# Units of 384 tokens for the third product of a fused float32r kernel, with a*b in pieces of 384 and 192 columns

## The chip, the cores and the metric

The kernel runs on one core of one Trainium2 chip. The metric is the device time of one execution in microseconds, lower is better. The chip is driven by five engines: TensorE (PE; its weight loads are listed apart as PEld), VectorE (DVE), ScalarE (ACT), GpSimd (POOL) and SyncE (SP), whose queue issues most of the DMAs.

## The reference

Three stages follow each other. Attention with 32 packed queries gives x of 8 batches of 576 tokens (4608 tokens in all) by 512 features; then a gated product, then a leaky one:

```
p_packed = softmax(p k^T / 8) v
x   = softmax(q p_packed^T / 8) p_packed
x   = ((x w1) * (x w2)) w3 w_out
h   = x w_in
out = max(0.01 h, h) w_out2
```

The products with d_ff = 1024 and 2048 are in float32.

## The kernel before

Tokens lie along the free dimension. W13 = w3 w_out (1024 x 512) is made once at the start. Float32 precision comes from float32r pairs: a number is split into hi (a cast on ACT) and lo = x - hi (a subtraction on DVE), and `three` (L128 to L130) issues three matmuls for a product: hi*hi, hi*lo, lo*hi. Each of these matmuls has a weight load of 128 x 128 ahead of it.

The first part runs batch by batch. Of batch b:

- **a*b** (`ab_unit`): 16 pieces, 8 blocks fc of 128 hidden features times two halves th of 288 tokens. A piece is 12 matmuls of 288 columns, M (weights) by AT (moving): 6 into one PSUM tile (a), 6 into another (b). ACT copies a to SBUF (`ab_a`), DVE multiplies (`ab_mul`), ACT casts hi (`ab_hi`), DVE subtracts (`ab_lo`). PSUM has four tiles `mm`, so two pieces are in flight.
- **x2** (`x2_unit`): for each half th four units e, each 24 matmuls (8 blocks fc, three passes) of 288 columns, W13 by ab. ACT copies the result to `x2s` and stores it to `x2d` in DRAM (`x2_store`).
- Beside these 16 + 8 slots (`slots`) stand the steps of attention for batch b+1 (`attention`: loads, scores s1 at slot 1, transposes at 7, pv at 10, pp at 13, scores s2 at 16, the softmax s2 and the split of AT at 16 to 21, and at 21 `m_pair`, the first two M = w pp of the next batch, on PE, cast on ACT and subtracted on DVE), the conversion of w_in and w_out2 from float64 words (`pump`, `conv_flush`), and staging.
- **Staging** (`stage_att`, L546 to L552 in `form`): for a unit of 768 tokens and one half a of the features it loads four tiles from `x2d` into buffers `v`, forms sums and hi and lo parts of seven operands (11 DVE operations, 7 casts on ACT into two buffers `P`), and stores them to `xfd` with 14 DMAs. One stage stands in each of the batches 2 to 6.

The second part (from L775 in `run`) multiplies the staged forms by w_in and w_out2, in matmuls of 384 columns, in a scheme of seven products.

Batch 0 follows an order written out by hand (`SCRIPT`); from batch 1 on the instructions are recorded in the order of the slots, and a scheduler places them on each engine. Each engine and each DMA queue then works its list in order: an instruction that waits holds those behind it.

Of the kernel before, what the change touches and what calls it, by code (L numbers as in the profile page):

```python
# [36 lines left out]
F32 = mybir.dt.float32  # L37
F32R = mybir.dt.float32r
# [17 lines left out]
def tile_kernel(ctx, tc, qT, kT, vL, pT, w12, w3b, wo1, win, wo2, out):  # L56
    nc = tc.nc
# [4 lines left out]
    x2d = dram.tile([P, 4, NT], F32, name="x2d")  # L62
# [17 lines left out]
    def ps_mm():  # L80
        return psum["pool"].tile([P, 512], F32, tag="mm", name="mm", bufs=3 if psum["early"] else 4)
# [11 lines left out]
    main = stA.enter_context(tc.tile_pool(name="main", bufs=1, side="right"))  # L93
# [5 lines left out]
    W13 = main.tile([P, 8, 2, DM], F32R, name="W13")  # L99
# [138 lines left out]
    def s2_mm(b):  # L238
        s2q[b] = scores(ppT[b % 2], "q", b)
# [151 lines left out]
    Mp, Mt, abp, ab32, abt, x2p = {}, {}, {}, {}, {}, {}  # L391
    mark = {"a": [], "v": []}
# [13 lines left out]
        m = Mt[b, f]  # L406
        sub(nc.vector, m[:, 1], Mp.pop((b, f)), m[:, 0])

    def half_tile(th):
        return main.tile([P, 2, TH], F32R, tag=f"ab{th}", name="ab", bufs=8)  # L410

    def ab_mm(b, fc, th):
        m = Mt[b, fc // 2]
        pair = ps_mm(), ps_mm()
        for w in range(2):
            c = fc % 2 * 256 + w * P
            for g in range(2):
                at = ATs[b, g]
                three(
                    pair[w][:, :TH], lambda i: m[:, i, g, c:c + P], lambda i: at[:, i, th * TH:(th + 1) * TH],  # L420
                    g == 0, g == 1,
                )
        abp[fc, th] = pair

    def ab_a(fc, th):
        pa, pb = abp[fc, th]
        a = main.tile([P, TH], F32, tag="a", name="a", bufs=2)
        nc.scalar.copy(a, pa[:, :TH])
        abp[fc, th] = a, pb

    def ab_mul(fc, th):
        a, pb = abp.pop((fc, th))
        t = main.tile([P, TH], F32, tag="ab32", name="ab32", bufs=3)
        nc.vector.tensor_tensor(out=t, in0=pb[:, :TH], in1=a, op=ALU.mult)  # L434
        ab32[fc, th] = t

    def ab_hi(fc, th):
        t = half_tile(th)
        mark["a"].append(nc.scalar.copy(t[:, 0], ab32[fc, th]))  # L439
        abt[fc, th] = t  # L440

    def ab_lo(fc, th, engine=nc.vector):
        t = abt[fc, th]
        mark["v"].append(sub(engine, t[:, 1], ab32.pop((fc, th)), t[:, 0]))

    def x2_mm(b, th, e):
# [4 lines left out]
        x2p[b, th, e] = ps  # L451

    def x2_store(b, th, e):
        t = main.tile([P, TH], F32, tag="x2s", name="x2s", bufs=2)
        nc.scalar.copy(t, x2p.pop((b, th, e))[:, :TH])
        nc.scalar.dma_start(out=x2d[:, e, b * S + th * TH:b * S + (th + 1) * TH], in_=t)

    AB = [(2 * f + n, th) for f in range(4) for th in range(2) for n in range(2)]
    X2 = [(th, e) for th in range(2) for e in range(4)]

    def m_pair(b, f):
        m_mm(b, f)
        m_mm(b, f + 1, False)
        for x in (f, f + 1):
            m_hi(b, x)
            m_lo(b, x)

    def ab_unit(b, fc, th):
# [106 lines left out]
    def stage_att(u, a):  # L575

        def tile(tag, bufs):
            return lambda: att.tile([P, HT], F32, tag=tag, name=tag, bufs=bufs)

        return stage(u, a, tile("v", VB), tile("PT", 2), lambda: tile("P", 2)().bitcast(F32R))  # L580

    def spread(steps, first, last):
        d = {}
        for n, f in enumerate(steps):
            d.setdefault(first + n * (last - first + 1) // len(steps), []).append(f)
        return d
# [13 lines left out]
        "U": x2_mm, "Us": x2_store, "P": ps_late,  # L600
# [25 lines left out]
    for b in range(1, 7):
        staging = {}
        if b in STAGE:
            steps = stage_att(*STAGE[b])
            staging = spread(steps[1:], 16, 23)  # L630
            staging[12] = steps[:1]
        slots(enumerate(pieces(b)), rest_of_m(b), attention(b + 1), pumps(PUMPS[b]), staging)
# [228 lines left out]
    for t in range(TB):  # L861
# [29 lines left out]
        if end:  # L891
# [3 lines left out]
            if t + 1 < TB:  # L895
                n = len(evicted)
# [45 lines left out]
```

## Time and profile before

| | before |
|---|---|
| time, median of 3 runs | 1265.77 us (1264.15 to 1268.5) |
| profiled execution, its own time | 1268.98 us |
| its span, first to last instruction | 1266.2 us |
| TensorE busy (share of the span) | 1245.5 us (98%) |
| weight loads busy | 1167.7 us (92%) |
| VectorE busy | 871.2 us (69%) |
| ScalarE busy | 610.4 us (48%) |
| GpSimd busy | 112.9 us (9%) |
| granted TensorE clock, mean | 0.999 |
| HBM traffic | 222 GB/s over the span |

Busy is the time in which at least one instruction of the engine was running. A matmul's recorded duration holds its latency, so consecutive matmuls overlap in the records; what one costs in a stream is read from starts, as the chain view gives it (a stretch divided by its count). Batches 1 to 6 lie between about 143 and 508 us of the span.

### The profile page before, as it was taken

Reading aid. Unit: us, or ns where it says so; the run is one execution under the profiler, and the core shown is the slowest. Engines: PE = TensorE matmul, PEld = TensorE weight load, DVE = VectorE, ACT = ScalarE, POOL = GpSimd, SP = SyncE. Lnnn points to the kernel's source line nnn. Section 1 sums busy time; section 2 is a strip of 40 time slices with the busy share of each in tenths; the row PEclk is TensorE's granted clock in tenths of the full one; section 3 lists DMA queues with packets and bytes.
Section 4 is the critical chain, followed back from the end, with each engine's and each line's share of the span. In section 5 each row is a group of like instructions: output and inputs, shape, how many; then the busy total and the mean of one; then the engine's idle time right before and its main releaser. Section 6 shows DMA issues by size and latency. Waiting matters only on the chain.

```text
span 1266.2 us, 23462 instructions
## 1 busy us (share of the span) xinstructions
PE 1245.5 (98%) x8984; PEld 1167.7 (92%) x8984; DVE 871.2 (69%) x1448; ACT 610.4 (48%) x1125; POOL 112.9 (9%) x136
## 2 busy tenths in 40 slices
PE   7989999999999999999999999999999999999998
PEld 2458898989889999999999999999999999999998
DVE  7887465767675767639866773886467448776667
ACT  4354345454545454546655655563433434443433
POOL 6553011111120200000000000000000000000000
PEclk9999999999999999999999999999999999999999
DMA  9954253767583835468788777284744674698883
GB/s 366 352 186 138 69 175 126 243 195 255 169 277 113 286 119 173 148 223 295 251 304 308 278 268 241 96 294 184 275 147 177 225 250 149 231 346 293 297 294 126
DMA packets 139952, 283.09 MB, mean 224 GB/s; under 512 B 14912, under 2 KB 67136, under 8 KB 139840
## 3 DMA queue, kind: packets, MB, share of 16 engines
q1 hardware_dynamic: 130624, 272.16, 61.9%
q10 hardware_dynamic: 9216, 9.44, 2.2%
q8 instruction: 70, 1.15, 0.4%
q14 instruction: 42, 0.34, 0.1%
HBM read 202.38 MB, written 79.17 MB: 222 GB/s over the span
## 4 chain that ended last, share of the span: by engine, by line
PE 94%; DMA 4%; DVE 1%; issue 0%; ACT 0%; SPq 0%; DVEq 0%; ACTq 0%
PE mm L130 31%; PE b L775 31%; PE c L775 16%; PE a L775 8%; PE at L164 3%; PE mm L379 3%; DMA c<-w3b 1%; DMA v<-x2d 1%; PE at L221 1%; DMA M<-w3b 1%; PE at L204 1%; DMA xl<-xfd 0%; DVE cT L283 0%; DMA c<-w 0%; DVE ct L280 0%
## 5 line engine op out<-in xcount | busy, mean ns | idle before, releaser
L130 PEld LDWEIGHTS mm<-AT,M 128*128 128x128 f32 x1536 | 205.5, 188 | 16.8 <-ACT ab L439 10.0
L130 PE MATMUL mm<-AT,M 128*128 128x288 f32 x1536 | 215.4, 297 | 3.4 <-DVE M L135 1.5
L775 PE MATMUL b<-xh,wi 128*128 128x384 f32 x768 | 216.6, 335 | 0.0
L775 PE MATMUL b<-gh,wo 128*128 128x384 f32 x768 | 215.1, 335 | 0.0
L130 PEld LDWEIGHTS mm<-ab,W 128*128 128x128 f32 x1536 | 203.7, 188 | 9.5 <-issue 6.1
L130 PE MATMUL mm<-ab,W 128*128 128x288 f32 x1536 | 207.8, 295 | 0.0
L775 PEld LDWEIGHTS b<-xh,wi 128*128 128x128 f32 x768 | 140.5, 188 | 0.0
L775 PEld LDWEIGHTS b<-gh,wo 128*128 128x128 f32 x768 | 140.4, 188 | 0.0
L775 PE MATMUL b<-xl,wi 128*128 128x384 f32 x384 | 128.4, 334 | 0.0
L775 PE MATMUL b<-gl,wo 128*128 128x384 f32 x384 | 128.3, 334 | 0.0
L550 ACT CAST gh<-gr 128x1152 fp32r<-128x1152 f32 (+1 forms) x72 | 75.7, 1053 | 77.5 <-PE b L775 48.0
L775 PE MATMUL c<-gh,wo 128*128 128x384 f32 x384 | 106.4, 334 | 0.0
L775 PE MATMUL c<-xh,wi 128*128 128x384 f32 x384 | 105.3, 334 | 0.0
L135 DVE TENSOR_TENSOR gl<-gr,gh 128x1152 fp32r<-128x1152 f32 (+1 forms) x72 | 87.9, 1220 | 15.8 <-ACT gh L550 15.8
L434 DVE TENSOR_TENSOR ab<-mm,a 128x288 f32<-128x288 f32 x128 | 58.0, 455 | 52.4 <-PE mm L130 32.8
L727 DVE TENSOR_TENSOR o<-b,o 128x384 f32<-128x384 f32 x108 | 59.3, 553 | 33.8 <-PE b L775 33.5
L550 ACT CAST gh<-gs 128x1152 fp32r<-128x1152 f32 (+1 forms) x54 | 56.9, 1054 | 45.7 <-PE b L775 27.2
L439 ACT CAST ab<-ab 128x288 fp32r<-128x288 f32 x128 | 55.4, 433 | 47.9 <-DVE ab L434 47.7
L735 ACT COPY gr<-b 128x384 f32<-128x384 f32 x96 | 45.9, 480 | 66.8 <-PE b L775 66.6
L721 ACT ACTIVATE gr<-gr 128x1152 f32<-128x1152 f32 (+1 forms) x54 | 57.3, 1061 | 42.3 <-DVE gr L727 42.1
L135 DVE TENSOR_TENSOR ab<-ab,ab 128x288 fp32r<-128x288 f32 x119 | 54.7, 459 | 32.2 <-ACT ab L439 30.7
L775 PEld LDWEIGHTS b<-xl,wi 128*128 128x128 f32 x384 | 72.1, 188 | 0.0
(119 smaller groups left out, 2045.7 us busy)
## 6 DMA issues: line engine op xcount, KB each, us to landing
xh<-xfd SPq DMA_DIRECT2D x126, 384.0 KB, 5.5
xl<-xfd SPq DMA_DIRECT2D x126, 384.0 KB, 5.2
part<-o SPq DMA_DIRECT2D x48, 384.0 KB, 2.7
o<-part SPq DMA_DIRECT2D x48, 384.0 KB, 6.4
xfd<-xt SPq DMA_DIRECT2D x49, 192.0 KB, 3.0
xfd<-xr SPq DMA_DIRECT2D x49, 192.0 KB, 3.0
raw<-kT SPq DMA_DIRECT2D x32, 288.0 KB, 5.3
raw<-qT SPq DMA_DIRECT2D x32, 288.0 KB, 4.0
```

The costliest lines, as they stand in the source:

```text
L130: ins = nc.tensor.matmul(dst, lhs(i), rhs(j), start=first and n == 0, stop=last and n == 2)
L135: return engine.tensor_tensor(out=out, in0=x, in1=rd(hi), op=ALU.subtract)
L164: ins = nc.tensor.matmul(dst(h)[c * 32:c * 32 + 32], lhs[r, c, :], rhs(c)[r], start=True, stop=True)
L204: together(nc.tensor.transpose(t[:, 0, c * P:(c + 1) * P], pt[:, c:512:4], ident), g + c == 0)
L379: nc.tensor.matmul(w13p[fc], words["3", i][:, c:c + P], words["o", jc], start=w13n[fc] == 1, stop=w13n[fc] == 8)
L434: nc.vector.tensor_tensor(out=t, in0=pb[:, :TH], in1=a, op=ALU.mult)
L439: mark["a"].append(nc.scalar.copy(t[:, 0], ab32[fc, th]))
L550: gate("a", nc.scalar.copy(hi[step], x[step]))
L721: nc.scalar.activation(out=out, in_=x, func=AF.Prelu, alpha=0.01)
L727: evicted.append(nc.vector.tensor_tensor(**args))
L735: nc.scalar.copy(out, ps)
L775: ins = nc.tensor.matmul(dst, lhs(l), rhs(r), start=first and n == 0, stop=last and n == total - 1, skip_group_check=True)
```

## The change

Batches 1 to 6 are 3456 tokens, nine units of 384. x2 is now computed per unit: one unit in batches 1, 3 and 5 (the first 384 of their tokens), two in batches 2, 4 and 6 (the rest of the batch before with the first 192 of this one, then the last 384). a*b is cut to fit: an odd batch into pieces of 384 and 192 columns, an even one into 192 and 384. An odd batch so has 16 + 4 slots, an even one 16 + 8. Attention for the next batch, the pumps and `m_pair` are moved to earlier slots in odd batches. Staging is taken out of odd batches; batch 4 and batch 6 have two stages. AT has two buffers in place of four; `x2s` shares three buffers with `a`. Batches 0 and 7 keep halves of 288.

```
-        at = main.tile([P, 2, S], F32R, tag="AT", name="AT", bufs=4)
+        at = main.tile([P, 2, S], F32R, tag="AT", name="AT", bufs=2)
...
+    WIDE = 384
+    CUTS = {b: ((0, 384, 576) if b % 2 else (0, 192, 576)) if 0 < b < 7 else (0, 288, 576) for b in range(B)}
...
+    def piece_of(b, fc, th):
+        c0, c1 = CUTS[b][th:th + 2]
+        if 0 < b < 7:
+            unit, at = divmod((b - 1) * S + c0, WIDE)
+        else:
+            unit, at = (b, th), 0
+        if unit not in sets:
+            sets[unit] = sides[0], {}
+            sides[0] ^= 1
+        side, tiles = sets[unit]
+        if fc not in tiles:
+            tiles[fc] = half_tile(side)
+        return tiles[fc], slice(at, at + c1 - c0)
...
     def ab_mm(b, fc, th):
...
+        c0, c1 = CUTS[b][th:th + 2]
...
-                    pair[w][:, :TH], lambda i: m[:, i, g, c:c + P], lambda i: at[:, i, th * TH:(th + 1) * TH],
+                    pair[w][:, :c1 - c0], lambda i: m[:, i, g, c:c + P], lambda i: at[:, i, c0:c1],
...
-        a = main.tile([P, TH], F32, tag="a", name="a", bufs=2)
+        a = main.tile([P, WIDE], F32, tag="a", name="a", bufs=3)[:, :n]
...
+    def x2_mm(unit, e):
+        n = TH if isinstance(unit, tuple) else WIDE
         ps = ps_mm()
         for fc in range(8):
-            t = abt[fc, th]
-            three(ps[:, :TH], lambda i: W13[:, fc, i, e * P:(e + 1) * P], lambda i: t[:, i], fc == 0, fc == 7)
+            t = sets[unit][1][fc]
+            three(ps[:, :n], lambda i: W13[:, fc, i, e * P:(e + 1) * P], lambda i: t[:, i, :n], fc == 0, fc == 7)
...
+    def units(b):
+        if b % 7 == 0:
+            return [(b, 0), (b, 1)]
+        return [3 * (b // 2)] if b % 2 else [3 * (b // 2) - 2, 3 * (b // 2) - 1]
...
+        first = 14 if short else 16
...
-        d[16] += [lambda: s2_mm(b)]
+        d[first] += [lambda: s2_mm(b)]
...
-        d[21] += [lambda: m_pair(b, 0)]
+        d[18 if short else 21] += [lambda: m_pair(b, 0)]
...
-        for s in (5, 10, 14, 18, 20, 22)[:n]:
+        for s in ((5, 9, 12, 15, 17, 19) if short else (5, 10, 14, 18, 20, 22))[:n]:
...
-    PUMPS = (0, 6, 6, 6, 5, 5, 4)
-    STAGE = {2: (0, 0), 3: (0, 1), 4: (1, 0), 5: (1, 1), 6: (2, 0)}
+    PUMPS = (0, 6, 5, 6, 4, 6, 5)
+    STAGE = {2: ((0, 0),), 4: ((0, 1), (1, 0)), 6: ((1, 1), (2, 0))}
...
+        short = b % 2 == 1
...
+            first, last = ((16, 19), (20, 23))[n]
+            staging.setdefault((12, 19)[n], []).extend(steps[:1])
```

Over the whole program the float32r matmuls of batches 1 to 6 were 2304 of 288 columns (1152 of a*b, 1152 of x2); they are now 576 of 384 and 576 of 192 in a*b, and 864 of 384 in x2. On PE, from the last pieces of batch 1 to the first of batch 2 (`ppT` and `raw` are the scores s2, `w` and `ppT` the M of the next batch), before:

```order
L130 MATMUL mm<-AT,M 128x288 x36
L130 MATMUL mm<-ab,W_76 128x288 x24
L164 MATMUL at<-raw,ppT_77 32x288 x16
L130 MATMUL mm<-ab,W_76 128x288 x120
L164 MATMUL at<-w,ppT_77 32x512 x16
L130 MATMUL mm<-ab,W_76 128x288 x48
L130 MATMUL mm<-AT,M 128x288 x24
```

and now:

```order
L130 MATMUL mm<-AT,M 128x384 x12
L130 MATMUL mm<-AT,M 128x192 x12
L164 MATMUL at<-raw,ppT_77 32x288 x16
L130 MATMUL mm<-AT,M 128x192 x12
L130 MATMUL mm<-ab,W_76 128x384 x72
L164 MATMUL at<-w,ppT_77 32x512 x16
L130 MATMUL mm<-ab,W_76 128x384 x24
L130 MATMUL mm<-AT,M 128x192 x12
```

Between the scores and the next batch stood 120 + 48 matmuls of 288 columns and the M; now 12 of 192, 72 + 24 of 384 and the M.

On DVE in batch 4, where the first sum of a stage (`PT<-v`) stands after the multiplication of the first piece behind pv, before:

```order
L434 TENSOR_TENSOR ab_4527<-mm,a 128x288
L135 TENSOR_TENSOR ab<-ab_4527,ab 128x288
L546 TENSOR_TENSOR PT<-v 128x384
L434 TENSOR_TENSOR ab_4549<-mm,a 128x288
L135 TENSOR_TENSOR v<-v,P 128x384
```

and now:

```order
L457 TENSOR_TENSOR ab_4230<-mm,a 128x384
L582 TENSOR_TENSOR PT<-v 128x384
L457 TENSOR_TENSOR ab_4252<-mm,a 128x192
L135 TENSOR_TENSOR v<-v,P 128x384
L135 TENSOR_TENSOR ab<-ab_4230,ab 128x384
```

The sum stands at the same place, between the multiplications of the first and the second piece.

On DVE at the end of batch 4, from the last steps of the softmax s2 to the first a*b of batch 5, before:

```order
L258 TENSOR_TENSOR sT<-sT,st_4766 128x576
L260 STREAM_TRANSPOSE a_4762<-sT 128x576
L135 TENSOR_TENSOR AT<-a_4762,AT 128x576
L260 STREAM_TRANSPOSE a_4858<-sT 128x576
L280 TENSOR_SCALAR cT<-c_4607 128x512
L283 SCALAR_TENSOR_TENSOR cT<-c_4607,cT 128x512
L135 TENSOR_TENSOR AT<-a_4858,AT 128x576
L135 TENSOR_TENSOR M<-at,M 128x1024 x2
L434 TENSOR_TENSOR ab_5017<-mm,a 128x288
```

and now:

```order
L582 TENSOR_TENSOR PT<-v,PT 128x384
L582 TENSOR_TENSOR v<-v 128x384
L135 TENSOR_TENSOR AT<-a_4475,AT 128x576
L135 TENSOR_TENSOR PT<-PT,P 128x384
L260 STREAM_TRANSPOSE a_4588<-sT 128x576
L135 TENSOR_TENSOR AT<-a_4588,AT 128x576
L582 TENSOR_TENSOR PT<-v,PT 128x384
L135 TENSOR_TENSOR PT<-PT,P 128x384
L135 TENSOR_TENSOR v<-v,P 128x384 x3
L135 TENSOR_TENSOR PT<-PT,P 128x384
L135 TENSOR_TENSOR M<-at,M 128x1024 x2
L457 TENSOR_TENSOR ab_4759<-mm,a 128x384
```

The second stage of batch 4 now stands around the split of AT and ahead of the subtractions of M.

## Rows read from the trace of the kernel before

**Rows 1.** The page: engines (busy us, share, instructions); a group's row (count, busy, mean ns).

```profile
PE 1245.5 (98%) x8984; PEld 1167.7 (92%) x8984; DVE 871.2 (69%) x1448; ACT 610.4 (48%) x1125; POOL 112.9 (9%) x136
...
L130 PE MATMUL mm<-AT,M 128*128 128x288 f32 x1536 | 215.4, 297 | 3.4 <-DVE M L135 1.5
```

**Rows 2.** Windows, about one batch each: stretch, length, busy by engine, PEclk, DMA, GB/s.

```profile
231.00:291.50 60.50, 60.50 (x604) 55.30 (x603) 43.77 (x85) 31.52 (x70) 9.23 (x12) 1.00 0.66 215
...
352.00:414.00 62.00, 60.98 (x607) 55.64 (x606) 41.79 (x83) 31.30 (x70) 8.39 (x11) 1.00 0.60 200
414.00:474.80 60.80, 60.37 (x602) 55.03 (x602) 41.54 (x83) 30.81 (x68) 7.72 (x10) 1.00 0.61 200
```

**Rows 3.** Waits of PE from 170 to 535 us: total, times, longest.

```profile
PE mm L130 <- DVE ab L434: 1.5, 2, 1.0
```

**Rows 4.** The chain, batch 2's x2 and batch 3's a*b: start us, length us, what, count.

```profile
240.18 16.09 PE mm L130 x120
...
280.82 0.47 PE at L204 x4
281.29 0.11 PE at L205
281.40 0.48 PE at L204 x4
...
281.99 4.76 PE mm L130 x36
...
291.38 0.11 PE at L233
```

**Rows 5.** The chain in the second part, a stream of 384 columns.

```profile
842.43 3.12 PE b L775 x18
```

**Rows 6.** Timeline of TensorE where a stream begins again: start, length, engine, what.

```profile
281.72 0.19 PEld L130 LDWEIGHTS mm<-AT,M 128*128 128x128 f32 x1
...
281.75 0.38 PE L130 MATMUL mm<-AT,M 128*128 128x288 f32 x1
...
281.83 0.32 PEld L130 LDWEIGHTS mm<-AT,M 128*128 128x128 f32 x2
```

**Rows 7.** Timeline of DVE, then PE, behind pv of batch 4.

```profile
350.25 0.46 DVE L434 TENSOR_TENSOR ab<-mm,a 128x288 f32<-128x288 f32 x1 [0.47 <-PE mm L130]
...
354.26 0.56 DVE L546 TENSOR_TENSOR PT<-v 128x384 f32<-128x384 f32 x1 [2.59 <-DMA v<-x2d]
354.73 0.45 DVE L434 TENSOR_TENSOR ab<-mm,a 128x288 f32<-128x288 f32 x1
...
355.24 1.87 PE L130 MATMUL mm<-AT,M 128*128 128x288 f32 x12 [1.02 <-DVE ab L434]
```

**Rows 8.** The chain at the same place: pv, then the load of staging.

```profile
347.10 1.25 PE at L221 x80
...
349.25 4.98 DMA v<-x2d
```

**Rows 9.** Groups of DVE from 170 to 535 us: count, busy us, mean ns.

```profile
L434 DVE TENSOR_TENSOR ab<-mm,a 128x288 f32<-128x288 f32 x99 | 45.0, 455 | 43.9 <-PE mm L130 28.0 <-ACT ab L439 10.6 <-ACT a L428 5.1
...
L135 DVE TENSOR_TENSOR v<-v,P 128x384 fp32r<-128x384 f32 x20 | 16.1, 825 | 0.7 <-ACT P L550 0.2
...
L135 DVE TENSOR_TENSOR PT<-PT,P 128x384 fp32r<-128x384 f32 x15 | 8.3, 554 | 1.4 <-ACT P L550 1.4
```

**Rows 10.** DMA issues of staging's hi parts: count, size, median us to landing.

```profile
xfd<-P SPq DMA_DIRECT2D x35, 192.0 KB, 3.3
```

**Rows 11.** Windows from scores s2 to next a*b, batches 1 (no staging) and 2.

```profile
179.40:203.70 24.30, 24.30 (x208) 22.72 (x201) 15.46 (x26) 8.65 (x15) 3.92 (x3) 1.00 0.53 171
240.20:264.50 24.30, 24.30 (x200) 22.75 (x201) 20.73 (x33) 10.20 (x18) 5.33 (x8) 1.00 0.89 288
```

**Rows 12.** Timeline of DVE, then ACT, end of batch 4: M of batch 5.

```profile
382.20 2.36 DVE L135 TENSOR_TENSOR M<-at,M 128x1024 fp32r<-128x1024 f32 x2 [2.90 <-ACT M L402]
...
381.15 1.94 ACT L402 CAST M<-at 128x1024 fp32r<-128x1024 f32 x2 [0.40 <-ACT x2s L455]
```

More of the change, by code (lines that the diff above doesn't have):

```diff
@@ L407, in m_lo, with half_tile @@
         sub(nc.vector, m[:, 1], Mp.pop((b, f)), m[:, 0])
-    def half_tile(th):
-        return main.tile([P, 2, TH], F32R, tag=f"ab{th}", name="ab", bufs=8)
+    WIDE = 384
+    CUTS = {b: ((0, 384, 576) if b % 2 else (0, 192, 576)) if 0 < b < 7 else (0, 288, 576) for b in range(B)}
+    def half_tile(side):
+        return main.tile([P, 2, WIDE], F32R, tag=f"ab{side}", name="ab", bufs=8)
+    sets, sides = {}, [0]
+    def piece_of(b, fc, th):
[11 more added lines that the diff above has]
+        return tiles[fc], slice(at, at + c1 - c0)
     def ab_mm(b, fc, th):
@@ L419, in ab_mm @@
                 three(
-                    pair[w][:, :TH], lambda i: m[:, i, g, c:c + P], lambda i: at[:, i, th * TH:(th + 1) * TH],
+                    pair[w][:, :c1 - c0], lambda i: m[:, i, g, c:c + P], lambda i: at[:, i, c0:c1],
                     g == 0, g == 1,
                 )
-        abp[fc, th] = pair
+        abp[fc, th] = pair, c1 - c0, b
     def ab_a(fc, th):
-        pa, pb = abp[fc, th]
-        a = main.tile([P, TH], F32, tag="a", name="a", bufs=2)
-        nc.scalar.copy(a, pa[:, :TH])
@@ L429, in ab_a @@
-        abp[fc, th] = a, pb
+        (pa, pb), n, b = abp[fc, th]
+        a = main.tile([P, WIDE], F32, tag="a", name="a", bufs=3)[:, :n]
+        nc.scalar.copy(a, pa[:, :n])
+        abp[fc, th] = a, pb, b
     def ab_mul(fc, th):
[L432 to L435, printed above, removed]
+        a, pb, b = abp.pop((fc, th))
+        n = a.shape[1]
@@ L437, in ab_hi @@
+        t = main.tile([P, WIDE], F32, tag="ab32", name="ab32", bufs=3)[:, :n]
+        nc.vector.tensor_tensor(out=t, in0=pb[:, :n], in1=a, op=ALU.mult)
+        ab32[fc, th] = t, b
     def ab_hi(fc, th):
-        t = half_tile(th)
-        mark["a"].append(nc.scalar.copy(t[:, 0], ab32[fc, th]))
-        abt[fc, th] = t
+        x, b = ab32[fc, th]
+        t, s = piece_of(b, fc, th)
+        mark["a"].append(nc.scalar.copy(t[:, 0, s], x))
+        abt[fc, th] = t[:, :, s]
     def ab_lo(fc, th, engine=nc.vector):
@@ L443, in ab_lo @@
         t = abt[fc, th]
-        mark["v"].append(sub(engine, t[:, 1], ab32.pop((fc, th)), t[:, 0]))
-    def x2_mm(b, th, e):
+        mark["v"].append(sub(engine, t[:, 1], ab32.pop((fc, th))[0], t[:, 0]))
+    def x2_mm(unit, e):
+        n = TH if isinstance(unit, tuple) else WIDE
         ps = ps_mm()
         for fc in range(8):
-            t = abt[fc, th]
-            three(ps[:, :TH], lambda i: W13[:, fc, i, e * P:(e + 1) * P], lambda i: t[:, i], fc == 0, fc == 7)
-        x2p[b, th, e] = ps
@@ L453, in x2_store @@
[L453 to L456, printed above, removed]
-    AB = [(2 * f + n, th) for f in range(4) for th in range(2) for n in range(2)]
-    X2 = [(th, e) for th in range(2) for e in range(4)]
+            t = sets[unit][1][fc]
+            three(ps[:, :n], lambda i: W13[:, fc, i, e * P:(e + 1) * P], lambda i: t[:, i, :n], fc == 0, fc == 7)
@@ new lines, in x2_mm, with x2_store, order_of @@
+        x2p[unit, e] = ps[:, :n]
+    def x2_store(unit, e):
+        n = TH if isinstance(unit, tuple) else WIDE
+        c = unit[0] * S + unit[1] * TH if isinstance(unit, tuple) else S + unit * WIDE
+        t = main.tile([P, WIDE], F32, tag="a", name="x2s", bufs=3)[:, :n]
+        nc.scalar.copy(t, x2p.pop((unit, e)))
+        nc.scalar.dma_start(out=x2d[:, e, c:c + n], in_=t)
+    AB = [(2 * f + n, th) for f in range(4) for th in range(2) for n in range(2)]
+    def order_of(b):
+        if b % 7 == 0:
+            return AB
+        return [(2 * f + n, th) for f in range(4) for n, th in (((0, 0), (0, 1), (1, 0), (1, 1)) if f < 3 else ((0, 0), (1, 0), (0, 1), (1, 1)))]
@@ L461, in m_pair @@
+    def units(b):
+        if b % 7 == 0:
+            return [(b, 0), (b, 1)]
+        return [3 * (b // 2)] if b % 2 else [3 * (b // 2) - 2, 3 * (b // 2) - 1]
     def m_pair(b, f):
@@ L473, in ab_unit, with x2_unit @@
         ab_lo(fc, th)
-    def x2_unit(b, th, e):
-        x2_mm(b, th, e)
-        x2_store(b, th, e)
+    def x2_unit(unit, e):
+        x2_mm(unit, e)
+        x2_store(unit, e)
     def pieces(b):
-        return [lambda x=x: ab_unit(b, *x) for x in AB] + [lambda x=x: x2_unit(b, *x) for x in X2]
+        return [lambda x=x: ab_unit(b, *x) for x in order_of(b)] + [lambda u=u, e=e: x2_unit(u, e) for u in units(b) for e in range(4)]
     def slots(pieces, *beside):
@@ L487, in slots, with attention @@
                     f()
-    def attention(b):
+    def attention(b, short):
         d = {s: [] for s in range(24)}
+        first = 14 if short else 16
         d[0] += [lambda: load_v(b, 0)]
@@ L506, in attention @@
         d[13] += [lambda: pp_mm(b), lambda: pp_copy(b)]
-        d[16] += [lambda: s2_mm(b)]
+        d[first] += [lambda: s2_mm(b)]
         for g in range(2):
-            s = 16 + 2 * g
+            s = first + (1 if short else 2) * g
             d[s] += [lambda g=g: s2_max(b, g)]
@@ L512, in attention @@
             d[s + 2] += [lambda g=g: s2_norm(b, g)]
-            d[s + 3] += [lambda g=g: s2_hi(b, g), lambda g=g: s2_lo(b, g)]
-        d[21] += [lambda: m_pair(b, 0)]
+            d[max(16, s + 3)] += [lambda g=g: s2_hi(b, g), lambda g=g: s2_lo(b, g)]
+        d[18 if short else 21] += [lambda: m_pair(b, 0)]
         if b + 1 < B:
-            d[17] += [lambda: load_p(b + 1), lambda: load_kq("k", b + 1, 0)]
-            d[19] += [lambda: load_kq("k", b + 1, 1)]
+            d[16 if short else 17] += [lambda: load_p(b + 1), lambda: load_kq("k", b + 1, 0)]
+            d[17 if short else 19] += [lambda: load_kq("k", b + 1, 1)]
         return d
@@ L615, in tile_kernel, with pumps @@
     conv_fetch()
-    def pumps(n, first=7):
+    def pumps(n, short):
         d = {}
-        for s in (5, 10, 14, 18, 20, 22)[:n]:
+        for s in ((5, 9, 12, 15, 17, 19) if short else (5, 10, 14, 18, 20, 22))[:n]:
             d[s] = [pump]
@@ L622, in pumps @@
         return d
-    PUMPS = (0, 6, 6, 6, 5, 5, 4)
-    STAGE = {2: (0, 0), 3: (0, 1), 4: (1, 0), 5: (1, 1), 6: (2, 0)}
+    PUMPS = (0, 6, 5, 6, 4, 6, 5)
+    STAGE = {2: ((0, 0),), 4: ((0, 1), (1, 0)), 6: ((1, 1), (2, 0))}
     for b in range(1, 7):
+        short = b % 2 == 1
         staging = {}
[L628 to L632, printed above, removed]
+        for n, ua in enumerate(STAGE.get(b, ())):
+            steps = stage_att(*ua)
+            first, last = ((16, 19), (20, 23))[n]
+            staging.setdefault((12, 19)[n], []).extend(steps[:1])
+            for k, f in spread(steps[1:], first, last).items():
+                staging.setdefault(k, []).extend(f)
+        slots(enumerate(pieces(b)), rest_of_m(b), attention(b + 1, short), pumps(PUMPS[b], short), staging)
     conv_flush()
```

2 lines of the change are left out of this document (1 added, 1 removed).

## The prediction

> **What bounds the kernel now.** I read the engines' totals first, then windows of about a batch each, then who made TensorE wait, then the chain for the price of one matmul, and last the places where the change takes cover away.
>
> TensorE is busy for 98% of the span [rows 1], and in a window of a whole batch for all of it, at a granted clock of 1.00, the level of 2.4 GHz [rows 2]. In the batches 1 to 6 it waited for another engine only twice, 1.5 us in all [rows 3]; the two windows with a gap show it, 60.98 of 62.00 and 60.37 of 60.80. DVE is busy for 41 to 44 us of a batch of 60, ACT for 31 [rows 2]. So the time of these batches is a number of matmuls times a price, and the change pays if it lowers that sum. Cover for the other engines matters only where it runs out.
>
> **The price of a matmul by its columns.** In a stream, 36 matmuls of 288 columns took 4.76 us, 132.2 ns each (120 took 16.09 us, 134.1 ns, one new start included) [rows 4]; 18 of 384 columns took 3.12 us, 173.3 ns [rows 5]. The line through the two is 0.428 ns a column with 9 ns to spare, and gives 91.1 ns at 192 columns. No matmul of 192 stands in the trace, so I bound it. The bound below is the line, 91.1. The bound above comes from the shortest full-width matmuls there are, transposes of 128 columns with a weight load of their own: four took 0.47 or 0.48 us, 118 to 120 ns each, and single ones 0.11 us [rows 4]. On the line they would take 64 ns. So a short matmul does not get cheaper with its columns; something else paces it, and one place shows what [rows 6]: where a stream of float32r begins anew, the second weight load starts 0.11 us after the first (281.72 and 281.83), and the first matmul, recorded at 281.75, is 0.38 us long, where such a matmul has 0.297 on the mean [rows 1]: for the 0.08 more it stood waiting, until about the second load's start. I read this as follows: a load begins only once the matmul ahead has taken its weights, and takes some 0.11 us before its own matmul can begin. At 288 and 384 columns that hides behind 132 and 173 ns; behind 91 ns it does not. I take **110 ns** for 192 columns, from the rows of float32r loads and single transposes, which are nearest in kind (the loads are the very ones that a*b issues), and keep 91 and 120 as ends.
>
> The Trainium skill, "TensorE: Matmul & The Clock Gate", section "LDWEIGHTS (loading the stationary operand)", gives a load of P columns as P / 1.2 ns, 107 ns for 128 columns, and so speaks against the change. By it the sum below would be 1.7 us less. The trace agrees: 0.11 us [rows 6].
>
> **The change part by part.**
>
> x2: 1152 matmuls of 288 become 864 of 384. 1152 x 132.2 = 152.3 us, 864 x 173.3 = 149.7 us: **-2.6 us** (the same columns, fewer fixed parts).
>
> a*b: 1152 of 288 become 576 of 384 and 576 of 192. 576 x 173.3 = 99.8 us, 576 x 110 = 63.4 us, 163.2 against 152.3: **+10.9 us**. At 91.1 ns it is 0.0 us, at 120 ns +16.6.
>
> Both together **+8.3 us**, from -2.6 to +14.0. It breaks even at 95.5 ns for 192 columns.
>
> Eviction of a*b: a piece of 384 and one of 192 in place of two of 288. DVE takes 455 ns at 288 and 554 at 384 [rows 9], 356 on that line at 192, and 554 + 356 = 2 x 455. The shortest time for an eviction is now 1.32 us (a piece of 192) in place of 1.59, with 554 ns for the multiplication of 384 that must end in it. Nothing. ACT stores 36 results in place of 48, off the path. The two buffers of AT hold back the cast of the next AT until the last a*b of the batch, which stands a dozen microseconds ahead of it on PE. Nothing.
>
> Staging behind pv: the first sum of a stage stands in DVE's list between the multiplications of the first and second piece behind pv, before and after. In batch 4 it started at 354.26 after 2.59 us of idle time, because its load, issued as pv ended, took 4.98 us; the next multiplication ended so late that PE idled 1.02 us [rows 7, 8]. From pv's end to the point where PE needs that tile there were 3.5 pieces of 1.59 and the pp transpose, 5.66 us; now 2.08 + 1.32 + 0.11 + 1.32 + 1.04 = 5.87 us, and the multiplication is 0.1 us shorter. So such a stall shrinks by 0.3 us, and can come in three batches, not five. Two of five stalled, for 1.5 us; I take one of three, 0.7: **-0.8 us**, between -1.5 and +0.6.
>
> The end of odd batches: from the scores to the next a*b PE now has 12 x 0.110 + 72 x 0.1733 + 1.88 (M) + 24 x 0.1733 = 19.8 us, where it had 24.3. DVE's work there was 15.46 us [rows 11], plus 0.7 for the last piece, 16.2. Behind M, PE had 48 matmuls of x2, 6.3 us; now 24, 4.2 us. The cast of the first M ends 0.97 us after it starts and its subtraction 1.18 us later [rows 12], some 2.3 us behind M. It fits; nothing.
>
> The end of batches 4 and 6: a second stage is added, 4 sums and 3 subtractions of 0.55 us and 4 subtractions of 0.83 [rows 9], 7.2 us of DVE. The fullest such window of before had 20.73 [rows 11], so 27.9, against 120 x 0.1733 + 1.88 + 48 x 0.1733 = 31.0 us of PE. It fits with 3 us to spare; nothing is added, but this is the tightest place. Its loads stand on SP's queue behind the four loads of K for the batch after next and behind stores of the first stage, which free their buffers. The pumps are 32 before and after.
>
> Sum: +8.3 - 0.8 = **+7.5 us**. The profiled execution took 1268.98 us (span 1266.2 and 2.8 around it), 3.2 above the median of the runs; with the change it would take 1276.5, and the median 1265.77 becomes **1273.3 us**.
>
> **The rivals.**
>
> A, faster: the loads of weights hide behind 192 columns too, and the price is on the line, 91.1 ns. The mechanism is the next load going ahead while the matmul runs; it decides below 95.5 ns. For it speaks that PEld is busy for only 92% of the span and that the transposes are plain float32, another kind; against it the loads [rows 6], which are float32r. Then -2.6 - 0.8: 1262.4 us. The Trainium skill, same page, section "Back-to-back issue gap", states about 81 ns for each pair of load and matmul at 128 columns, which would be this rival; it also states 131 ns at 512, and the trace has 173 at 384 [rows 5], so the trace bears it out badly.
>
> B, slower still: the second stage in batches 4 and 6 is late. Its seven casts share two buffers P, each free only when its store has landed, 3.3 us [rows 10], and DVE and ACT work in order, so the subtractions of AT and M wait behind it. Two such waits beyond the 3 us to spare cost 3.6 us at each of the two ends; the point is where the first M is subtracted later than 31.0 us behind the scores. +7.2: 1280.5 us.
>
> C, no change: a load can begin some ten nanoseconds before its predecessor's matmul starts, the price is near 98 ns, and what a*b loses (4.0 us) x2 and staging give back (3.4): 1266.4 us.
>
> That the change would not do what it says is excluded by the order of the instructions: the counts of matmuls are those above.
>
> **How the numbers follow.** About 0.3%, 3.8 us, is what a measurement of this kernel can tell from no change. Forecast 0.67, between 106 and 120 ns with the staging term at either end: 1270 to 1281, slower throughout. A 0.16, of which 0.09 is over 0.3% faster (the stalls go as well) and 0.07 within. B 0.11, slower. C 0.06, within. So faster 0.09, same 0.13, slower 0.78. The range leaves out the faster part of A and the far end of B: 1263 to 1283.
>
> **What would show it.** Right: in the chain 12 matmuls of 192 columns in some 1.3 us, six streams of 384 in x2 at 173 ns, batches 1 to 6 longer by 7 to 8 us with TensorE busy throughout. Wrong: pieces of 192 in 1.1 us or less (A); waits of PE for DVE's AT or M where batch 5 or 7 begins (B). If pieces of 192 take over 1.45 us, the upper bound was not one.

## The result, and the profile after

The median went from 1265.84 us to **1276.27 us** (six runs each; 1274.18 to 1278.5 after): the ratio is 1.0079, with a 95% interval of 1.0067 to 1.0091. The change makes the kernel slower by 10.4 us. The profiled execution after took 1275.71 us, its span 1273.9.

The page after, to be set against [rows 1]: engines, then the costliest group of matmuls.

```profile
PE 1253.7 (98%) x8696; PEld 1175.8 (92%) x8696; DVE 872.7 (69%) x1448; ACT 607.4 (48%) x1113; POOL 112.5 (9%) x136
...
L130 PE MATMUL mm<-AT,M 128*128 128x384 f32 (+2 forms) x1536 | 226.4, 305 | 1.9 <-DVE M L135 1.5
```

288 matmuls fewer, and 8 us more of busy TensorE. The shares are those of before to the per cent, 92% for the loads too: from the page alone nobody would see what happened. Windows by stage do show it. First those of before, then of after, each time batches 1 to 6, batch 7 and the second part (columns as in [rows 2]):

```profile
143.50:508.20 364.70, 363.25 (x3620) 332.49 (x3620) 249.50 (x491) 184.73 (x409) 48.96 (x61) 1.00 0.58 189
508.20:561.00 52.80, 52.80 (x417) 51.25 (x417) 32.30 (x67) 26.42 (x63) 0.00 (x0) 1.00 0.51 172
561.00:1266.20 705.20, 700.92 (x4034) 700.04 (x4032) 483.73 (x722) 335.99 (x533) 0.00 (x0) 1.00 0.69 243
```

```profile
141.20:513.00 371.80, 371.80 (x3332) 340.86 (x3331) 252.25 (x491) 183.51 (x397) 48.07 (x61) 1.00 0.56 184
513.00:565.80 52.80, 52.80 (x418) 51.25 (x417) 32.28 (x67) 26.39 (x63) 0.00 (x0) 1.00 0.54 181
565.80:1273.90 708.10, 702.34 (x4034) 699.75 (x4032) 483.30 (x722) 334.12 (x533) 0.00 (x0) 1.00 0.69 242
```

Batches 1 to 6 take 7.1 us more. The idle time of TensorE there, 1.45 us before (364.70 less 363.25), is gone: the batches are longer because the matmuls themselves take more time. Batch 7, which is unchanged, takes the same. The second part takes 2.8 us more from its first matmul to the end (2.9 by these rounded borders), though its instructions stand in the same order; that was not in the sum. What lies ahead of batch 1 was 2.3 us shorter in this execution (141.2 against 143.5); another execution of before has 140.8, so this varies by itself. In the first profile of before the granted clock stood at 0.50 from 39.17 to 42.58 us, which it did neither in the second nor after; matmuls in that stretch lost some 1.6 us.

The chain after, in batch 5 (start, length, what, count), beside [rows 4]:

```profile
357.81 21.02 PE mm L130 x120
...
407.54 5.54 PE mm L130 x36
```

120 matmuls of x2 at 384 columns in 21.02 us are 175 ns each, with a new start. The 36 of a*b are 24 of 384 and 12 of 192. If a matmul of 384 is at 175.5, the mean over all pairs found below, the 12 of 192 took 5.54 - 4.21 = 1.33 us, 111 ns each. Neither this 1.33 us nor 175 ns is on the side of rival A.

### The profile page after: what moved, and what is told of

It is laid out like the page before. It is cut to its first block, busy times and chain, and to the rows that moved or that the text cites. A ratio compares the mean times of both kernels' runs of the same rounds, so it can differ in the third digit from the quotient of the medians.

```text
span 1273.9 us, 22809 instructions
## 1 busy us (share of the span) xinstructions
PE 1253.7 (98%) x8696; PEld 1175.8 (92%) x8696; DVE 872.7 (69%) x1448; ACT 607.4 (48%) x1113; POOL 112.5 (9%) x136
## 4 chain that ended last, share of the span: by engine, by line
PE 93%; DMA 5%; DVE 1%; SPq 0%; issue 0%; ACT 0%; DVEq 0%; ACTq 0%
PE mm L130 32%; PE b L814 30%; PE c L814 15%; PE a L814 8%; PE at L164 3%; PE mm L379 3%; DMA c<-w3b 1%; DMA xfd<-xt 1%; PE at L221 1%; DMA M<-wo 1%; DMA xl<-xfd 1%; DMA M<-w3b 1%; PE at L204 1%; DMA xfd<-xr 0%; DMA c<-w 0%
## 5 line engine op out<-in xcount | busy, mean ns | idle before, releaser
L130 PEld LDWEIGHTS mm<-AT,M 128*128 128x128 f32 x1536 | 216.8, 189 | 15.8 <-ACT ab L463 6.5
L130 PE MATMUL mm<-AT,M 128*128 128x384 f32 (+2 forms) x1536 | 226.4, 305 | 1.9 <-DVE M L135 1.5
L130 PEld LDWEIGHTS mm<-ab,W 128*128 128x128 f32 x1248 | 200.2, 188 | 8.1 <-issue 3.4
L130 PE MATMUL mm<-ab,W 128*128 128x384 f32 (+1 forms) x1248 | 204.9, 323 | 0.0
L457 DVE TENSOR_TENSOR ab<-mm,a 128x384 f32<-128x384 f32 (+2 forms) x128 | 58.0, 455 | 60.7 <-PE mm L130 41.2
L135 DVE TENSOR_TENSOR ab<-ab,ab 128x192 fp32r<-128x192 f32 (+2 forms) x119 | 59.2, 508 | 31.1 <-ACT ab L463 30.9
L463 ACT CAST ab<-ab 128x384 fp32r<-128x384 f32 (+2 forms) x128 | 55.5, 434 | 46.0 <-DVE ab L457 44.7
L450 ACT COPY a<-mm 128x384 f32<-128x384 f32 (+2 forms) x128 | 50.8, 397 | 52.1 <-PE mm L130 48.7
```

What stands on the lines that cost most here:

```text
L450: nc.scalar.copy(a, pa[:, :n])
L457: nc.vector.tensor_tensor(out=t, in0=pb[:, :n], in1=a, op=ALU.mult)
L463: mark["a"].append(nc.scalar.copy(t[:, 0, s], x))
```

## The experiments

Ten runs were made, two of them of the two kernels as they are. For each I give the stretches of its profile: batches 1 to 6, then the second part from its first matmul to the end (us), beside the median time and its ratio to the kernel before on the same chip. From the traces I also took the price of a matmul: the mean time from the start of one float32r matmul to the start of the next of the same width in batches 1 to 6 (some 500 pairs or more each; pairs with a wait or a new start between them, over some 50 ns above the median, are left out, and where the outliers are cut moves a price by about 1 ns).

### Two more profiles of the same kernels

One profile of each kernel can't tell which part of a difference of 3 us is chance, so both ran once more, with no edit.

> The kernel before, profiled a second time: 20 of its executions had a median of 1265.5 us, the profile shown of it 1269.0. Theory T (the profile caught an execution with waits that are not in most of them: the two of staging, 1.5 us in all, and a start 1.5 us longer): most batches at 60.35 us, batches 1 to 6 at 362.1 to 363.5 us, the start at 141 to 142.5 us, time 1264 to 1266 us; the change is then to be counted from 362 to 363 us. Theory R (the waits recur, the median is lower for another reason): batches 1 to 6 at 364 to 365 us again, with the waits behind pv in batches 4 and 5.

> The changed kernel, profiled a second time. Its second part took 708.0 us in the first profile, 2.8 us more than before, with the same instructions in the same order. Theory T (waits on transfers that wander from one execution to the next): another value between 705 and 708.5 us, with waits at other places; batches 1 to 6 at 371.8 us again. Theory W (the changed order of staging lengthens the second part): 707.5 to 708.5 us again, with the waits at the same places.

| profile | batches 1 to 6 | second part | span |
|---|---|---|---|
| before | 364.7 | 705.2 | 1266.2 |
| before, again | 364.2 | 705.9 | 1263.8 |
| after | 371.8 | 708.0 | 1273.9 |
| after, again | 372.7 | 707.0 | 1273.4 |

So the batches cost 7.1 to 8.5 us, and the second part 1.1 to 2.8, in each pairing. Where the latter comes from is in the waits of PE in the second part (total, times, longest), here of before, of after and of after again:

```profile
PE c L775 <- DMA xl<-xfd: 0.7, 1, 0.7
```

```profile
PE c L814 <- DMA xh<-xfd: 1.2, 1, 1.2
PE b L814 <- ACT o L774: 0.7, 1, 0.7
PE c L814 <- DMA xl<-xfd: 0.4, 1, 0.4
```

```profile
PE c L814 <- DMA xh<-xfd: 1.2, 1, 1.2
PE b L814 <- ACT o L774: 0.7, 1, 0.7
```

Both profiles of after wait at the same two places. I set the 4032 matmuls of the second part side by side by their number: after again falls behind before again by 0.7 us between the 1050th and the 1200th and by 0.7 us more between the 3000th and the 3150th, at these waits, and nowhere else. (The first profile of after loses another 1 us in small steps.) The first wait can be followed one step further, in ACT's timeline, after and then before again:

```profile
754.18 0.51 ACT L586 CAST xt<-xr 128x384 fp32r<-128x384 f32 x1 [2.40 <-DMA xfd<-xt]
754.59 0.47 ACT L774 COPY o<-b 128x384 f32<-128x384 f32 x1
```

```profile
744.87 0.51 ACT L550 CAST xt<-xr 128x384 fp32r<-128x384 f32 x1 [1.84 <-DMA xfd<-xt]
745.29 0.47 ACT L735 COPY o<-b 128x384 f32<-128x384 f32 x1
```

A cast of staging stands in ACT's list ahead of the copy that TensorE waits for. It waits for a store to free its buffer, and after the change 0.56 us longer. Why the store lands later there, and the load of `xh` near the end as well, stays open. The cut at 448 below, with staging as before, waits 1.3 us for `o` at this place too, so moved stages are not needed for such a wait. In the batches, the waits behind pv came again in the second profile of before (1.1 us): they are not of one execution alone.

### a*b cut elsewhere, x2 left alone

To get the price by columns, the kernel before was cut in a*b alone, at 384, 320 and 448 of the 576 columns:

```
+    def cut_of(b, th):
+        c = 384 if 0 < b < 7 else TH
+        return ((0, c), (c, S))[th]
...
-                    pair[w][:, :TH], lambda i: m[:, i, g, c:c + P], lambda i: at[:, i, th * TH:(th + 1) * TH],
+                    pair[w][:, :c1 - c0], lambda i: m[:, i, g, c:c + P], lambda i: at[:, i, c0:c1],
```

> The kernel before with nothing changed but the cut of a*b in batches 1 to 6: pieces of 384 and 192 columns in place of two of 288 (x2 stays in halves of 288, staging and slots stay). Theory F: 576 x (173.3 + 110 - 2 x 132.2) ns = +10.9 us, batches 1 to 6 at 375.6 us, time 1276.7 us, more than the changed kernel. Theory S (short matmuls cost a fixed extra of some 19 ns over the line): the same here, +10.9 us. Theory M: no change, 364.7 us and 1265.8 us.

> As the run before, but cut at 320: pieces of 320 and 256 columns. Theory F: both lie above the floor (146 and 118.6 ns), 264.6 against 264.4 ns a pair, 0.1 us in all: batches 1 to 6 at 364.8 us, time 1265.9 us. Theory S: 19 ns for each of 576 matmuls of 256 columns, +11 us: 375.6 us, 1276.7 us. Theory M: no change.

> As the run before, but cut at 448: pieces of 448 and 128 columns. Theory F: 200.7 + 110 against 264.4 ns, +46.3 ns for each of 576 pairs, +26.7 us: batches 1 to 6 at 391.4 us, time 1292.5 us, with the price of 128 columns the same as that of 192. Theory S: 200.7 + 64 + 19, +11 us: 375.9 us, 1277 us, with 83 ns at 128 columns. Theory M: no change, unless evictions are late.

| cut | batches 1 to 6 | second part | median | ratio |
|---|---|---|---|---|
| 384 and 192 | 377.0 | 705.8 | 1279.42 | 1.0117 (1.0100 to 1.0135) |
| 320 and 256 | 367.1 | 705.9 | 1268.69 | 1.0027 (1.0015 to 1.0040) |
| 448 and 128 | 404.7 | 707.5 | 1307.65 | 1.0332 (1.0314 to 1.0350) |

The price of a matmul of a*b, from all kernels:

| columns | 128 | 192 | 256 | 288 | 320 | 384 | 448 |
|---|---|---|---|---|---|---|---|
| ns, all pairs | 111.7 | 110.3 | 119.5 | 132.6 | 146.6 | 175.5 | 204.8 |
| ns inside a piece, its first pair left out | 111.8 | 111.7 | 119.5 | 132.7 | 146.5 | 174.1 | 203.6 |
| on the line through 288 and 384 of the second row | 63.7 | 91.3 | 118.9 | | 146.5 | | 201.7 |

The two rows differ by what happens where the width changes. In the change, the first pair of a piece of 384 behind a piece of 192 takes 199.3 ns (27 cases), and that of a piece of 192 behind one of 384 takes 87.4 (27 cases). Together that is 286.7 ns, about the 285.8 of one pair of each inside the pieces, so both rows give the same sum.

From 256 columns up the price inside a piece lies within 2 ns of a line of 0.431 ns a column with 8.5 ns to spare, close to the prediction's 0.428 and 9. At 128 and 192 it is the same, some 112 ns. The floor meets the line near 240 columns. Chains of the cuts at 320 and at 448, streams of the short pieces alone:

```profile
216.41 2.81 PE mm L130 x23
```

```profile
223.29 2.61 PE mm L130 x23
```

23 matmuls of 256 columns took 2.81 us, 23 of 128 columns 2.61: half the columns, 7% less time.

With the cut at 384 the sum for a*b is 576 x (174.7 + 110.8) - 1152 x 132.6 = +11.7 us (its own prices), and the batches took 12.3 to 12.8 more. The cut at 320 gives +0.5 by prices, and took 2.4 to 2.9 more: 0.8 of that is a wait for DVE, 0.5 is x2, whose matmuls took 132.5 ns here for 132.1, and the rest I can't place. The cut at 448 gives +29.5; of the 10.5 to 11 us beyond, 6.0 are waits (5.3 for ACT's copy of a), and what the granted clock took besides is told in the last section.

### x2 in units of 384, a*b as before

The other half of the change alone: units of 384 and the staging of the change, with a*b in pieces of 288, whose results are cast in two parts where a piece lies in two units.

```
-    CUTS = {b: ((0, 384, 576) if b % 2 else (0, 192, 576)) if 0 < b < 7 else (0, 288, 576) for b in range(B)}
+    CUTS = {b: (0, 288, 576) for b in range(B)}
...
-    def piece_of(b, fc, th):
+    def parts_of(b, fc, th):
...
+        for t, p in abt[fc, th]:
+            mark["a"].append(nc.scalar.copy(t[:, 0], x[:, p]))
```

> The changed kernel with a*b of batches 1 to 6 back in halves of 288 columns (casts and subtractions of a half split where a unit of 384 ends); x2, staging, slots and buffers as in the change. Theory F (a floor of weight loads: a matmul of N columns costs the larger of 9 + 0.428 N ns and 110 ns): a*b costs what it cost before, x2 keeps its 2.6 us, the two stalls of staging go: batches 1 to 6 take 364.7 - 2.6 - 1.5 to 364.7 - 2.6, so 360.6 to 362.1 us, and the time is 1262 to 1263 us, below both kernels. Theory M (the moved steps, the fewer slots and the doubled stages cost the time, by waits, not the columns): 371 to 372 us as in the changed kernel, time 1276 us.

The time is 1265.29 us, ratio 0.9993 (0.9981 to 1.0005): no difference from before, and 11.0 us below the change. Expected were 1262 to 1263 us. The batches came as expected, the time did not: the second part was longer, and the granted clock was below 1.000 on the mean in 8 of its 12 executions. The four at 1.000 took 1261.5 to 1263.6 us, the ten such executions of before on that chip 1263.6 to 1266.2; with so few this is a hint and no more. Its windows:

```profile
142.70:503.70 361.00, 360.97 (x3332) 329.45 (x3332) 255.56 (x539) 186.47 (x445) 48.37 (x61) 1.00 0.57 190
```

The batches gain 3.2 to 3.7 us: 2.1 by the price of x2 (864 x 173.7 - 1152 x 132.1) and the rest by waits that are gone. The second part took 706.6. The cut of a*b is what loses the time: with it undone the 11.0 us are gone, and the batches are 10.8 us shorter than those of the change.

### Weight loads of 64 columns for the pieces of 192

That the floor is a weight load was read from one place where a stream begins [rows 6]. To test it, the pieces of 192 got loads of 64 columns in place of 128, with the same number of matmuls and moving columns. The kernel then leaves out the results of the other 64 features of these pieces and sets them to zero:

```
+        rows = 64 if c1 - c0 == 192 else P
...
-                    pair[w][:, :c1 - c0], lambda i: m[:, i, g, c:c + P], lambda i: at[:, i, c0:c1],
+                    pair[w][:rows, :c1 - c0], lambda i: m[:, i, g, c:c + rows], lambda i: at[:, i, c0:c1],
...
+            nc.gpsimd.memset(rd(t[r:, :, s]), 0.0)
```

> The changed kernel, but the a*b pieces of 192 columns compute only the first 64 of each block of 128 features, with weight loads of 64 columns (the other 64 rows of their results are set to zero by GpSimd; half of the work of these pieces is left out, the number of matmuls and their columns stay). Theory F (the load of 128 columns is the floor): the price of 192 columns falls from 110 to the line, 91 to 95 ns, and batches 1 to 6 from 371.8 to 361 to 363 us, time 1265 to 1268 us. Theory S (a floor of some other kind, such as issue, that does not hang on the load's columns): 110 ns as before, 371.8 us, 1276 us.

The price at 192 columns fell from 110.3 to 89.6 ns (inside a piece from 111.7 to 88.7, where the line has 91.3). Groups of weight loads in the batches, after and with half loads (count, busy, mean ns; the first row holds both widths of a*b):

```profile
L130 PEld LDWEIGHTS mm<-AT,M 128*128 128x128 f32 x1153 | 165.7, 190 | 10.1 <-issue 4.8 <-ACT ab L463 4.4
```

```profile
L130 PEld LDWEIGHTS mm<-AT,M 128*128 128x128 f32 x575 | 98.5, 188 | 5.9 <-ACT ab L469 3.9 <-DVE ab L460 1.0 <-ACT a L452 0.5
L130 PEld LDWEIGHTS mm<-AT,M 128*64 128x64 f32 x576 | 54.4, 135 | 6.7 <-ACT ab L469 3.9 <-issue 1.4
```

A load of half the columns is recorded 53 ns shorter, and the same chain stretch as above, 24 matmuls of 384 and 12 of 192, lost 0.25 us:

```profile
399.08 5.29 PE mm L130 x36
```

That is 12 x 21 ns, and all of it is the pieces of 192.

The starts in the trace show the load at work. Inside the pieces of 256 columns and more, the next load is recorded 2 to 3 ns after the start of the matmul ahead of it (median of each width). At 192 columns with full loads it is recorded 22 ns after it, at 128 columns 52 ns, and the loads follow each other at 111.7 ns: the loads lag, and a matmul, recorded as started, stands until its weights are there. With half loads the 22 ns are 3 ns again. A load of 64 columns also means results of 64 rows, and no run separates the two; that the load stops lagging speaks for the load.

The batches took 360.7 us in place of 371.8 to 372.7, and the median fell from 1276.27 to 1264.94, which is 0.9998 of the kernel before on its chip. In the second part this kernel was the slowest of all (709.9), again by waits of the two kinds, here 2.2 us for `o` and 1.9 for the loads.

### Staging moved, with a*b and x2 as before

AT with two buffers, the pumps and the stages of the change, in the kernel before; then the same without the stages:

```
-        at = main.tile([P, 2, S], F32R, tag="AT", name="AT", bufs=4)
+        at = main.tile([P, 2, S], F32R, tag="AT", name="AT", bufs=2)
...
-    PUMPS = (0, 6, 6, 6, 5, 5, 4)
-    STAGE = {2: (0, 0), 3: (0, 1), 4: (1, 0), 5: (1, 1), 6: (2, 0)}
+    PUMPS = (0, 6, 5, 6, 4, 6, 5)
+    STAGE = {2: ((0, 0),), 4: ((0, 1), (1, 0)), 6: ((1, 1), (2, 0))}
```

> The kernel before with only staging, the pumps and the two buffers of AT as in the change (no stage in batches 3 and 5, two in 4 and 6, PUMPS 6, 5, 6, 4, 6, 5); a*b and x2 in halves of 288. Theory F (the columns alone set the time, the moved steps are covered): batches 1 to 6 between 362.1 and 364.7 us, time between 1264 and 1266 us. Theory M (doubled stages hold back AT and M of the batches 5 and 7): waits of PE for DVE where they begin, batches 4 and 6 at 62 us or more, 366 us and 1268 us or more.

> The kernel before with only the two buffers of AT and the numbers of pumps of the change; one stage in each of the batches 2 to 6 as before. Tells which part of the run with staging alone cost its 3 us (1.5 to 2 in the batches, the rest in the second part). Theory D (the doubled stages do): batches 1 to 6 at 364 to 365 us, second part 705 to 706 us, time 1265 to 1266 us. Theory A (two buffers of AT, or the pumps, do): batches 366 us, time 1268 us.

| | batches 1 to 6 | second part | median | ratio |
|---|---|---|---|---|
| all three | 366.2 | 707.2 | 1268.39 | 1.0021 (1.0011 to 1.0030) |
| without the stages | 362.6 | 705.6 | 1265.33 | 0.9993 (0.9982 to 1.0004) |

So the buffers of AT and the pumps cost nothing, and the stages, in the kernel of halves, cost 3 us, in the batches and, in this one profile, in the second part. In the batches it is for the most part rival B. Waits of PE where all three were moved, then its DVE and PE where batch 5 begins:

```profile
PE mm L130 <- DVE M L135: 3.7, 3, 1.5
```

```profile
382.40 0.56 DVE L546 TENSOR_TENSOR PT<-v,PT 128x384 f32<-128x384 f32 x1 [1.80 <-DMA xfd<-PT]
383.93 1.22 DVE L135 TENSOR_TENSOR M<-at,M 128x1024 fp32r<-128x1024 f32 x1
```

```profile
385.21 1.58 PE L130 MATMUL mm<-AT,M 128*128 128x288 f32 x10 [1.53 <-DVE M L135]
```

1.5 of the 3.7 us come from the start of the program, as in every kernel. Another 1.5 are the mechanism that the rival described, though at a buffer PT and not at P: a stage's sum waits 1.80 us until its buffer's store has landed, the subtraction of M stands behind it on DVE, and TensorE waits for M. Two microseconds on, TensorE waits 0.6 us for ACT's copy of x2, which stands behind a cast of the stage that waited for the store of a P. The last 0.6 of the 3.7 us are of another kind, where batch 3 begins (PE, then ACT):

```profile
262.68 3.17 PE L130 MATMUL mm<-AT,M 128*128 128x288 f32 x22 [0.63 <-DVE M L135]
```

```profile
259.56 0.40 ACT L455 COPY x2s<-mm 128x288 f32<-128x288 f32 x1 [3.07 <-DMA x2d<-x2s]
```

There ACT's copy of x2 waited 3.07 us for a store of x2s, and the casts of M stood behind it. Whether the moved stages made that store late is not shown.

The kernel of halves has 24.3 us between scores and a*b [rows 11]. The change has 31.3 there (357.81 to 389.09), and no such wait.

### x2 in units of 384, five stages

Could the gain of x2 be kept without the cost in the second part? One stage in each batch, as before, on top of the x2-only kernel:

```
-    STAGE = {2: ((0, 0),), 4: ((0, 1), (1, 0)), 6: ((1, 1), (2, 0))}
+    STAGE = {2: (0, 0), 3: (0, 1), 4: (1, 0), 5: (1, 1), 6: (2, 0)}
...
+            staging = spread(steps[1:], *((13, 18) if short else (16, 23)))
```

> x2 in units of 384, a*b in halves of 288, and one stage in each of the batches 2 to 6 (in odd ones from slot 13 to 18), pumps 6, 4, 6, 4, 6 in the batches 2 to 6. Looks for a kernel below both. Theory D (doubled stages lengthen the second part by 1 to 2 us, and x2 gains 2.6 us in the batches): batches 361 to 362 us, second part 705 to 706 us, time 1262 to 1263.5 us. Rival (the short x2 of an odd batch, 16.6 us, doesn't cover a stage beside the split of AT and M): PE waits for DVE where the batches 4 and 6 begin, 1 to 4 us each, time 1265 to 1270 us.

No: 1269.22 us, ratio 1.0021 (1.0009 to 1.0034). The batches took 364.8 and waited again:

```profile
PE mm L130 <- DVE M L135: 2.7, 3, 1.5
PE c L818 <- ACT gh L592: 1.1, 1, 1.1
PE mm L130 <- DVE ab L462: 0.9, 1, 0.9
```

1.5 of the 2.7 us are again those of the start; the rest stand where batches 4 and 6 begin. In an odd batch with a single unit there is too little x2 behind M to cover a stage. The wait for `gh` is in the second part, which took 708.1. But this does not show that a stage in each batch costs the second part as much as doubled stages do, for right behind that wait the granted clock stood at 0.50 (columns as in the windows of the last section):

```profile
1096.85:1100.26 3.41, 3.41 (x12) 0.50 0.99 400
```

Matmuls of 384 columns started some 0.32 us apart there, in place of 0.17, which cost 1.7 us. Without it the second part would have taken some 706.4. What the doubled stages cost the second part stays open. No kernel of this study is faster than the one before by more than the spread of the runs.

## Why the prediction was right

It said slower, 1273.3 us with 1263 to 1283; it came to 1276.27. Step by step:

- **What bounds the batches: right.** TensorE is busy for all 371.80 us of them, and a number of matmuls times a price gives them: 864 x 173.7 - 1152 x 132.1 + 576 x (175.5 + 110.3) - 1152 x 132.6 = +9.7 us. Undisturbed batches show as much: 3 x (53.65 + 70.23) = 371.6 after, 6 x 60.35 = 362.1 before, +9.5.
- **The price of 192 columns: right,** 110.3 ns for 110 (111.7 inside a piece), and for the reason given: it falls to 89.6 with half the load, and does not fall at all from 192 to 128 columns. The Trainium skill, "TensorE: Matmul & The Clock Gate", section "LDWEIGHTS (loading the stationary operand)", gives P / 1.2, 107 ns, and so, as an estimate from it, 53 ns less for 64 columns; the floor of 110 to 112 ns agrees, and so do the 53 ns between the two kinds of loads.
- **x2 at -2.6: right** (-2.1). **a*b at +10.9: 1 us too low** (+11.9). The terms were mis-sized a little each: inside a piece a matmul of 192 columns costs 111.7 ns for 110 (1.0 us over 576) and one of 384 costs 174.1 for 173.3 (0.5 us), while 132.6 for 132.2 in the matmuls taken away gives 0.5 us back. Together the sum had +8.3 for what measured +9.7.
- **Staging behind pv at -0.8: right in kind, some 1 us too small.** The waits for DVE's `ab` in the batches of before were 1.5 us, and 1.1 in its second profile; after, none and 0.5. By the lengths of whole batches, the disturbed ones lost 2.6 and 2.2 us over the undisturbed before, and 0.2 and 1.1 after, on the mean 1.8 less. This missing 1 us made up for most of the 1.4 that the sum of the matmuls lacked, so it is in part luck that the forecast of +7.5 lies so near to what the batches took.
- **The end of odd batches: right,** no wait there.
- **The end of batches 4 and 6: no wait, but less to spare than said.** DVE after, end of batch 4:

```profile
380.78 0.56 DVE L582 TENSOR_TENSOR PT<-v,PT 128x384 f32<-128x384 f32 x1 [1.37 <-DMA xfd<-PT]
...
385.41 0.56 DVE L135 TENSOR_TENSOR PT<-PT,P 128x384 fp32r<-128x384 f32 x1 [1.30 <-ACT P L586]
...
386.64 2.36 DVE L135 TENSOR_TENSOR M<-at,M 128x1024 fp32r<-128x1024 f32 x2 [0.67 <-ACT M L402]
```

  The sum had added DVE's busy time. But DVE waits within that time, for a store and for ACT, and the first M was subtracted near 387.8, 1.3 us before batch 5's a*b began at 389.09, and the second by 389.0. Of the 3 us that all of DVE's work there was to leave, 0.1 us was left.
- **What the sum left out:** the second part, which it took as unchanged. It grew by 1.1 to 2.8 us, most of it at the two places above.

So the median's +10.4 is made of some 7.8 us in the batches (the mean of the two pairs of profiles) and 1.9 in the second part, against +7.5 forecast; the rest is within the spread of the runs.

Rival A fell: 192 columns would have cost 91 ns, and come near that only with loads of 64. The Trainium skill, "TensorE: Matmul & The Clock Gate", section "Back-to-back issue gap", by which a pair at 128 columns takes about 81 ns and one at 512 about 131, does not hold for these float32r pairs: 111.7 at 128, and 204.8 already at 448. Rival C fell with it. Rival B did not happen in the change, but its mechanism is real: it cost some 2 us (1.5 by DVE, 0.6 by ACT) where batch 5 begins and x2 was kept in halves.

## What to carry to other kernels

Where each matmul brings its own weights, price it as the larger of a line by its moving columns and the time of its load; here 0.431 ns a column plus 8.5, but never under some 111 ns. Cutting 576 columns as 384 + 192 rather than 2 x 288 therefore costs what the short piece lies above its line, some 20 ns each time, and the longer units of x2 gave back only 2.1 us of it. And take a price from pairs inside a stream: right behind a change of width the same matmul of 384 columns took 199 ns in place of 174, and one of 192 took 87 in place of 112.

## What the runs showed of the hardware

- **Short matmuls have a floor that their loads set.** 128 and 192 columns cost the same (111.8 and 111.7 ns inside a piece), the loads lag behind the matmuls there and not from 256 columns up, and 64 loaded columns in place of 128 took 21 ns off a matmul of 192. The busy share of loads does not show this: it was 92% before and after.
- **The granted clock halved behind waits, but not behind each.** With the cut at 448, TensorE waited four times for ACT in the batches:

```profile
244.87 0.89 PE L130 MATMUL mm<-AT,M 128*128 128x128 f32 x6 [1.29 <-ACT a L433]
312.31 1.54 PE L130 MATMUL mm<-AT,M 128*128 128x128 f32 x6 [1.98 <-ACT a L433]
381.80 0.89 PE L130 MATMUL mm<-AT,M 128*128 128x128 f32 x6 [1.22 <-ACT a L433]
450.55 0.89 PE L130 MATMUL mm<-AT,M 128*128 128x128 f32 x6 [0.85 <-ACT a L433]
```

  Windows of TensorE (stretch, length, busy, PEclk, DMA share, GB/s), around the second of these waits and behind the last two:

```profile
308.00:310.00 2.00, 2.00 (x19) 1.00 0.99 372
...
312.00:314.00 2.00, 1.69 (x7) 0.50 0.41 102
314.00:316.00 2.00, 2.00 (x10) 0.50 0.53 194
...
318.00:320.00 2.00, 2.00 (x40) 0.86 0.86 255
...
383.43:386.85 3.42, 3.42 (x16) 0.50 0.78 281
...
451.70:455.11 3.41, 3.41 (x17) 0.50 0.66 223
```

  The granted clock went from 1.00 (2.4 GHz) to 0.50 (1.2 GHz) at 311.75 us, within the wait of 1.98 us, and rose again at 318.58. It halved twice more, at 383.43 and at 451.70, behind waits of 1.22 us and of 0.72 and 0.85 us. The wait of 1.29 us in the same kernel and one of 1.25 us in the second part of the change left it at 1.00, so the length of one wait does not tell whether the clock falls. At 0.50 the matmuls of 128 columns started 213 ns apart, in place of 112, and those of 288 columns 240, in place of 132. That cost 2.9, 1.5 and 1.5 us in the three stretches, 5.9 us in all. With the 6.0 us of waits it accounts for what lay beyond the prices; the two together even come to 1 us more than that.
